# Transposes in rows of four, a gate ahead of the last product, and new due times in a planned convolution and MLP kernel

## The chip, the cores and the metric

The kernel runs on one core of a Trainium2 chip. Its time is the device time of one execution in microseconds, as the median of several runs. The profile comes from one more execution, taken by the hardware profiler. The engines are TensorE (PE; its weight loads are listed as PEld), VectorE (DVE), ScalarE (ACT), GpSimd (POOL) and SyncE (SP), which only starts transfers here.

## The reference

The input is a sequence of 2048 tokens with 640 channels. A layer norm with scale and shift goes into a gated long convolution (a short convolution of k by four taps, times v, then a causal convolution over all 2048 positions with a kernel for each channel, then times the normalised input), and its result is added to the input. A second layer norm with scale and shift goes into an MLP of width 1728 with a squared ReLU, whose result is gated and added:

```python
def _B_ref(x, w1, b1, w2, b2):
    h = jnp.einsum("bsd,df->bsf", x, w1) + b1
    zero = jnp.zeros_like(h)
    r = jnp.where(h > zero, h, zero)
    h = r * r
    out = jnp.einsum("bsf,fd->bsd", h, w2) + b2
    return out
...
h = _layernorm(x, axis=-1) * (1 + ca) + sa
x = x + ga * _A_ref(h, A_k, A_v, A_shift_k, A_ssm_k, A_ssm_D)
h = _layernorm(x, axis=-1) * (1 + cb) + sb
x = x + gb * _B_ref(h, B_w1, B_b1, B_w2, B_b2)
```

## The kernel before, in words

**Stages.** The convolution is done in five blocks of 128 channels, as transforms written as matrix products in float32. Its result x1 goes to DRAM (`x1_d`, in the trace `x_d`). The MLP follows. Its tokens are cut into eight chunks of 256 (n = 0 to 7), and two chunks form one of four pairs (s = 0 to 3). Every float32 operand of the MLP's products is split into a high and a low part of a faster float32 form (`split`: ACT copies the high part, DVE subtracts it), and a product is three matmuls (`l1`, 256 columns, and `l2`, 320 columns). A scheme with seven products in place of eight (sums and differences of blocks of the weights and the activations) saves matmuls in both layers. Layer one leaves its activations in DRAM (`h_d`); layer two loads them chunk by chunk, forms their differences, splits them into one of four buffers (in the trace `xp1r`, `ka`, `kz`, `xa`) and multiplies.

**The tokens** (`tokens`, `turned`). For each chunk x1 is loaded as two tiles of 128 tokens with 640 channels. They are normalised (`hat`), and each of the five blocks of 128 channels is transposed on PE: two transposes of 128x128 into one bank of PSUM (`xtp`), in two groups of their own, and one eviction by ACT (odd blocks) or DVE (even blocks), which applies scale and shift and writes the tile `xf`. From chunk 2 on the banks 6 and 7 serve for it. There are 80 such transposes.

**Layer two** (`second_layer`). In each chunk seven sums are built in seven banks (`ps7`, numbered 1 to 7), each from the six pairs of rows of the activations, p = 0 to 5; four of them (2, 4, 5 and 3) also get a remainder (rows a and c, with the bias). The result has four pieces: c[1,0] = ps2 + ps1, c[0,0] = ps4 + u3, c[0,1] = ps5 + u3 and c[1,1] = ps3 + u2, where u2 is first ps6 + ps1, u3 = ps7 + u2, and u2 then becomes ps5 + u2. Each piece is multiplied by the gate's row (`row0b`, in the trace `gbrow`), added to the residual (`xf` in the trace) and stored. In the last chunk, before, all four sums are formed first, and then the four pieces are gated, added and stored one after the other; c[1,1] is the last.

**What sets the order.** The program is first built as a graph of nodes, and a planner (`Graph.order`) then lays them on the engines: a simulated list schedule with a price for every node. On each engine the node that is ready and has the earliest due time goes next. The due times stand in a long table, `URGE`, in tenths of a microsecond with a minus sign, in the order in which the nodes of a kind are made; nodes of the MLP do not start earlier than a certain time before they are due. The instructions of each engine are then issued in this order, and on the chip each engine works its list strictly in this order, waiting for what an instruction needs. At most six transfers of SP are open at a time. For PE the planner prices a change of the form of a matmul (`ENTER`, `LEAVE`), where form was the number of rows and columns of the array in use, so that in the MLP before a transpose is no change of form. Only the order reaches the chip, no planned time does.

In the trace nearly all instructions carry the line L407, on which the planner issues them, so they are told apart by their tiles: `ps<-ident,x` and `ps<-ident,up` are the transposes of the tokens, `xf<-ps,cbs` their evictions, `ps<-t,w`, `ps<-xa,w`, `ps<-ka,w`, `ps<-kz,w` products of layer one, and `ps<-w,xp1r` and the like products of layer two.

## Time and profile before

| | us |
|---|---|
| median of 3 runs | 658.59 (658.23 to 659.29) |
| the profiled execution | 658.96 |
| its span | 657.2 |

The span runs from the first to the last instruction of the program in the profile; the execution's own time has 1.8 us more around it. The convolution takes PE up to about 280 us, layer one of the MLP up to about 477 us, layer two up to 652 us. "PE busy" counts matmuls as pipelined work with modelled ends, so durations of neighbours overlap; the cost of a matmul is read from one start to the next.

### The profile page before, as it was taken

Reading aid. Unit: us, or ns where it says so; the run is one execution under the profiler, and the core shown is the slowest. Engines: PE = TensorE matmul, PEld = TensorE weight load, DVE = VectorE, ACT = ScalarE, POOL = GpSimd, SP = SyncE. Lnnn points to the kernel's source line nnn. Section 1 sums busy time; section 2 is a strip of 40 time slices with the busy share of each in tenths; the row PEclk is TensorE's granted clock in tenths of the full one; section 3 lists DMA queues with packets and bytes.
Section 4 is the critical chain, followed back from the end, with each engine's and each line's share of the span. In section 5 each row is a group of like instructions: output and inputs, shape, how many; then the busy total and the mean of one; then the engine's idle time right before and its main releaser. Section 6 shows DMA issues by size and latency. Waiting matters only on the chain.

```text
span 657.2 us, 17277 instructions
## 1 busy us (share of the span) xinstructions
PE 629.6 (96%) x7012; PEld 584.4 (89%) x7012; DVE 516.1 (79%) x969; ACT 358.1 (54%) x681; POOL 226.8 (35%) x294
## 2 busy tenths in 40 slices
PE   7999999999999999899999999999989999999996
PEld 7888779878878878499999999999978999999996
DVE  1758848699978666886886787778899989788896
ACT  3554767885866775556585664456463424233321
POOL 1528649768786756311324200235400000000000
PEclk8999999999999999999999999999999999999999
DMA  9898989999896722563756632145555443553353
GB/s 223 217 272 284 267 231 249 208 234 216 229 241 164 142 56 72 156 208 89 213 152 194 193 112 75 56 140 166 159 147 171 151 137 118 166 176 120 114 157 81
DMA packets 143464, 111.00 MB, mean 169 GB/s; under 512 B 50836, under 2 KB 123348, under 8 KB 143384
## 3 DMA queue, kind: packets, MB, share of 16 engines
q1 hardware_dynamic: 141252, 109.28, 60.1%
q8 instruction: 55, 0.90, 0.6%
q10 hardware_dynamic: 2068, 0.61, 0.4%
q14 instruction: 25, 0.20, 0.1%
q0 software_dynamic: 64, 0.01, 0.0%
HBM read 79.99 MB, written 29.88 MB: 167 GB/s over the span
## 4 chain that ended last, share of the span: by engine, by line
PE 49%; DVE 3%; DMA 2%; ACT 1%; issue 1%; DVEq 0%; ACTq 0%
PE ps L407 49%; DMA up<-h_d 2%; DVE up L407 1%; DMA x<-x_d 1%; DVE w L407 0%; DVE ka L407 0%; DVE s L407 0%; DVE xp1r L407 0%; DVE kz L407 0%; ACT w L407 0%; ACT xf L407 0%; DVE xa L407 0%; DVE outs L407 0%; ACT kz L407 0%; ACT xa L407 0%
## 5 line engine op out<-in xcount | busy, mean ns | idle before, releaser
L407 PE MATMUL ps<-a,gb 128*64 128x128 f32 x1260 | 76.8, 275 | 3.3 <-ACT a L407 2.1
L407 PEld LDWEIGHTS ps<-a,gb 128*64 128x64 f32 x1260 | 69.3, 137 | 11.6 <-ACT a L407 5.4
L407 ACT ACTIVATE up<-ps,b1t 128x256 f32<-128x256 f32 (+1 forms) x112 | 50.6, 471 | 48.4 <-PE ps L407 46.4
L407 PE MATMUL ps<-t,w 128*128 128x256 f32 x504 | 72.7, 284 | 0.3 <-DVE up L407 0.3
L407 PEld LDWEIGHTS ps<-cst,p 64*64 64x64 f32 (+1 forms) x1792 | 60.7, 137 | 11.4 <-issue 6.1
L407 PE MATMUL ps<-cst,p 64*64 64x64 f32 (+1 forms) x1792 | 66.7, 247 | 3.9 <-POOL p L407 2.5
L407 PEld LDWEIGHTS ps<-t,w 128*128 128x128 f32 x504 | 64.8, 189 | 0.7 <-DVE up L407 0.5
L407 ACT ACTIVATE a<-ps 128x512 f32<-128x512 f32 x72 | 40.8, 620 | 31.9 <-PE ps L407 31.8
L407 DVE SCALAR_TENSOR_TENSOR up<-up 128x512 f32<-128x512 f32 (+2 forms) x70 | 45.3, 655 | 11.3 <-ACT up L407 10.6
L407 DVE TENSOR_TENSOR up<-up 128x256 f32<-128x256 f32 (+2 forms) x124 | 44.7, 383 | 7.4 <-DMA up<-h_d 5.7
L407 PE MATMUL ps<-xa,w 128*128 128x256 f32 x342 | 49.5, 284 | 0.0
L407 POOL TENSOR_TENSOR wm<-wm,wm 128x640 f32<-128x640 f32 x24 | 38.2, 1591 | 19.7 <-ACT wm L407 19.1
L407 PEld LDWEIGHTS ps<-xa,w 128*128 128x128 f32 x342 | 44.1, 190 | 0.4 <-DVE xa L407 0.2
L407 PE MATMUL ps<-w,xp1r 128*128 128x320 f32 x216 | 40.1, 310 | 1.9 <-ACT up L407 1.1
L407 PE MATMUL ps<-w,xa 128*128 128x320 f32 x216 | 41.1, 309 | 0.0
L407 PE MATMUL ps<-w,kz 128*128 128x320 f32 x216 | 39.9, 310 | 0.6 <-DVE kz L407 0.6
L407 PE MATMUL ps<-w,ka 128*128 128x320 f32 x216 | 40.4, 309 | 0.0
L407 DVE SCALAR_TENSOR_TENSOR kva<-ps,tap,kva 128x511 f32<-128x511 f32 (+2 forms) x48 | 35.8, 747 | 5.5 <-ACT kva L407 3.8
L407 DVE TENSOR_TENSOR up<-ps,up 128x256 f32<-128x256 f32 (+2 forms) x67 | 28.5, 435 | 13.4 <-PE ps L407 8.3
L407 PEld LDWEIGHTS ps<-w,xp1r 128*128 128x128 f32 x216 | 33.7, 188 | 2.6 <-ACT up L407 1.3
L407 PEld LDWEIGHTS ps<-w,kz 128*128 128x128 f32 x216 | 33.6, 188 | 1.0 <-DVE kz L407 1.0
L407 ACT ACTIVATE kz<-up 128x896 fp32r<-128x896 f32 (+2 forms) x24 | 16.8, 699 | 32.1 <-DVE up L407 31.8
(199 smaller groups left out, 1533.4 us busy)
## 6 DMA issues: line engine op xcount, KB each, us to landing
h_d<-up SPq DMA_DIRECT2D x51, 256.0 KB, 2.5
up<-h_d SPq DMA_DIRECT2D x48, 256.0 KB, 3.5
wm<-in_w_mod_dram SPq DMA_DIRECT2D x30, 320.0 KB, 5.2
w1s<-in_B_w_dram SPq DMA_DIRECT2D x25, 320.0 KB, 3.7
p<-in_A_ssm_k_dram SPq DMA_DIRECT2D x20, 256.0 KB, 4.4
p<-kv_d SPq DMA_DIRECT2D x20, 256.0 KB, 4.6
xp<-in_A_q_dram SPq DMA_DIRECT2D x10, 512.0 KB, 8.0
xf<-x_d SPq DMA_DIRECT2D x8, 640.0 KB, 4.1
```

Source lines behind the costliest of these rows:

```text
L407: fn(*real, **{k: a.real() if isinstance(a, View) else a for k, a in kw.items()})
```

## The change

It has three parts. First, from chunk 1 on, the blocks of a chunk's tokens are transposed as (0, 1), (2, 3) and (4): four transposes, or two for the last, as one node into one bank, which is then emptied by one eviction for each block. The form of a matmul in the MLP becomes the number of its entries in PE's queue, 4 for float32 and for transposes, 2 for the split products, and going from one to the other has a price in the planner, 0.040 and 0.085 us. Second, in the last chunk of layer two the pieces are gated as soon as their sums are there, and the last piece is taken apart: u2 is multiplied by the gate and added to the residual early, and ps3 is multiplied by the gate straight from its bank and added as the last step. `rest2` is the former inner loop as a function. Third, the table of due times is new: all of the MLP's, most of those of blocks 2 to 4 of the convolution, and some of blocks 0 and 1.

```diff
--- before.py
+++ after.py
@@ -30,8 +30,8 @@
 SPARE = 60.0
 
 FETCH = (3.6, 5.5)
-ENTER = {(64, 128): 0.104}
-LEAVE = {(64, 64): 0.11}
+ENTER = {(64, 128): 0.104, 4: 0.04, 2: 0.085}
+LEAVE = {(64, 64): 0.11, 4: 0.0, 2: 0.0}
 WINDOW = 10.24 / 3
 
 
@@ -679,10 +679,10 @@
     def mm(o, a, b, start, stop, hold=(), more=False):
         n = 2 if (isinstance(b, View) and b.buf.dtype == F32R) else 4
         ins = [x for x in (a, b) if isinstance(x, View)]
-        g.add("PE", 0.0, (nc.tensor.matmul, "matmul", (o, a, b), dict(start=start, stop=stop, **({"skip_group_check": True} if more else {}))), [o], ins, entries=n, hold=hold, form=(a.p[1] - a.p[0] if isinstance(a, View) else a.shape[0], o.p[1] - o.p[0]))
+        g.add("PE", 0.0, (nc.tensor.matmul, "matmul", (o, a, b), dict(start=start, stop=stop, **({"skip_group_check": True} if more else {}))), [o], ins, entries=n, hold=hold, form=(a.p[1] - a.p[0] if isinstance(a, View) else a.shape[0], o.p[1] - o.p[0]) if len(g.nodes) <= g.mlp else n)
 
     def turn(o, x, hold=()):
-        g.add("PE", 0.0, (nc.tensor.transpose, "transpose", (o, x, ident), {}), [o], [x] if isinstance(x, View) else [], entries=2, hold=hold, form=(P, P))
+        g.add("PE", 0.0, (nc.tensor.transpose, "transpose", (o, x, ident), {}), [o], [x] if isinstance(x, View) else [], entries=2, hold=hold, form=(P, P) if len(g.nodes) <= g.mlp else 4)
 
     def copy(eng, o, i, hold=()):
         if eng is act:
@@ -1220,19 +1220,23 @@
             out.append(o)
         return out
 
-    def turned(n, xh, b):
+    def turned(n, xh, bs):
         g.key = ("xt", n)
-        t = psum(f"xtp_{n}_{b}", (P, 2, P), XTB if n > 1 else (4, 5, 6, 7), **(one() if n > 1 else {}))
-        for i in range(2):
-            with g.as_one(0.11):
-                turn(t[:, i], xh[i][:, b * P : (b + 1) * P])
-        o = XF[n % 2][:, b]
-        t2 = t.rearrange("p i s -> p (i s)")
-        c1, c0 = cbs[:, 1, b : b + 1], cbs[:, 0, b : b + 1]
-        if b % 2:
-            act.activation(o, t2, AF.Identity, scale=c1, bias=c0)
-        else:
-            dve.tensor_scalar(o, t2, c1, c0, op0=ALU.mult, op1=ALU.add)
+        t = psum(f"xtp_{n}_{bs[0]}", (P, len(bs), 2, P), XTB if n > 1 else (4, 5, 6, 7), **(one() if n > 1 else {}))
+        turns = [(j, i) for i in range(2) for j in range(len(bs))]
+        for k in range(0, len(turns), len(turns) if n else 1):
+            some = turns[k:] if n else turns[k : k + 1]
+            with g.as_one(0.11 * len(some)):
+                for j, i in some:
+                    turn(t[:, j, i], xh[i][:, bs[j] * P : (bs[j] + 1) * P])
+        for j, b in enumerate(bs):
+            o = XF[n % 2][:, b]
+            t2 = t[:, j].rearrange("p i s -> p (i s)")
+            c1, c0 = cbs[:, 1, b : b + 1], cbs[:, 0, b : b + 1]
+            if b % 2:
+                act.activation(o, t2, AF.Identity, scale=c1, bias=c0)
+            else:
+                dve.tensor_scalar(o, t2, c1, c0, op0=ALU.mult, op1=ALU.add)
 
     def tokens(s, ks=(0, 1)):
         for k in ks:
@@ -1242,8 +1246,8 @@
             load_x1(n)
             stats2(n)
             xh = hat(n)
-            for b in range(NB):
-                turned(n, xh, b)
+            for bs in ((0, 1), (2, 3), (4,)) if n else ((b,) for b in range(NB)):
+                turned(n, xh, bs)
             if k == 0:
                 halves(n, T1[s])
 
@@ -1521,6 +1525,17 @@
             for i, (a, y) in enumerate(((0, 0), (0, 1), (1, 0))):
                 mm(acc, h[a], w[y], first and i == 0, last and i == 2)
 
+    def rest2(n, ps7, i):
+        k, o = {2: (1, 0), 4: (0, 0), 5: (0, 1), 3: (2, 1)}[i]
+        g.key = ("l2", n)
+        a, c = HS[n, "a"], HS[n, "c"]
+        wa, wc = W2S[NF - 2], W2S[NF - 1]
+        o = slice(320 * o, 320 * o + 320)
+        l2(ps7[i], parts(a, k), (wa[:, 0, o], wa[:, 1, o]), False, False)
+        with g.as_one(0.294):
+            mm(ps7[i], c[:, k], wc[:, 0, o], False, False)
+            mm(ps7[i], cone[n % 2][:, k], wc[:, 1, o], False, False)
+
     def second_layer(n):
         x = X2[n] = xres[n % 2]
         ps7 = {i: psum(f"c{i}_{n}", (P, 320), ANY, track=f"c{(7 * n + j) % 8}") for j, i in enumerate((1, 2, 6, 7, 4, 5, 3))}
@@ -1542,15 +1557,8 @@
                 wv = parts(w, b) if b < 6 else (e[:, 0], e[:, 1])
                 l2(ps7[i], parts(h, a), wv, p == 0, p == NP - 1)
             if p == 4:
-                g.key = ("l2", n)
-                a, c = HS[n, "a"], HS[n, "c"]
-                wa, wc = W2S[NF - 2], W2S[NF - 1]
-                for i, k, o in ((2, 1, 0), (4, 0, 0), (5, 0, 1), (3, 2, 1)):
-                    o = slice(320 * o, 320 * o + 320)
-                    l2(ps7[i], parts(a, k), (wa[:, 0, o], wa[:, 1, o]), False, False)
-                    with g.as_one(0.294):
-                        mm(ps7[i], c[:, k], wc[:, 0, o], False, False)
-                        mm(ps7[i], cone[n % 2][:, k], wc[:, 1, o], False, False)
+                for i in (2, 4, 5, 3):
+                    rest2(n, ps7, i)
             if p == 2:
                 g.key = ("lx2", n)
                 rows = x1_d.buf.real[n * CH : (n + 1) * CH, :].rearrange("(l p) d -> p l d", p=P)
@@ -1562,11 +1570,11 @@
         add(dve, c[:, 1, 0], ps7[2], e1)
         add(dve, u2, ps7[6], e1)
         add(dve, u3, ps7[7], u2)
-        add(dve, c[:, 0, 0], ps7[4], u3)
-        add(dve, u2, ps7[5], u2)
-        add(dve, c[:, 0, 1], ps7[5], u3)
-        add(dve, c[:, 1, 1], ps7[3], u2)
         if n < NC - 1:
+            add(dve, c[:, 0, 0], ps7[4], u3)
+            add(dve, u2, ps7[5], u2)
+            add(dve, c[:, 0, 1], ps7[5], u3)
+            add(dve, c[:, 1, 1], ps7[3], u2)
             for i in range(2):
                 t = c[:, i].rearrange("p k d -> p (k d)")
                 mul(dve, t, t, row0b)
@@ -1574,477 +1582,480 @@
             for a in range(2):
                 sp_dma(osrc[a, :, 2 * n : 2 * n + 2], x[64 * a : 64 * a + 64], 5120)
             return
-        for i, k in ((1, 0), (0, 0), (0, 1), (1, 1)):
+
+        def gated(i, k, t, done=True):
             o = slice(320 * k, 320 * k + 320)
-            mul(dve, c[:, i, k], c[:, i, k], row0b[:, o])
+            mul(dve, c[:, i, k], t, row0b[:, o])
             add(dve, x[:, i, o], x[:, i, o], c[:, i, k])
-            for a in range(2):
+            for a in range(2) if done else ():
                 (act_dma if a else sp_dma)(osrc[a, :, 2 * n + i, o], x[64 * a : 64 * a + 64, i, o], 1280)
 
+        gated(1, 0, c[:, 1, 0])
+        add(dve, c[:, 0, 0], ps7[4], u3)
+        gated(0, 0, c[:, 0, 0])
+        add(dve, u2, ps7[5], u2)
+        gated(1, 1, u2, False)
+        add(dve, c[:, 0, 1], ps7[5], u3)
+        gated(0, 1, c[:, 0, 1])
+        gated(1, 1, ps7[3])
+
     URGE = {
...
-        ("hat", 0): [-1183, -2159],
+        ("hat", 0): [2106, -32],
...
+        ("l2", 7): [-6306, -5775, -7408, -6254, -6504, -5644, -6237, -8084, -5259, -5995, -7115, -6238, -6310, -6026,
+            -6324, -6350, -6191, -6322, -6400, -6434, -7376, -6077, -6318, -6221, -6411, -6487, -6320, -6275, -5914,
+            -6078, -6349, -5864, -7141, -6229, -7236, -6205, -6317, -7217, -7128, -6343, -6013, -6351, -6279, -6050,
+            -6223, -6030, -6160, -6511, -6402, -5611],
...
-        ("lw2", 0): [-3968],
...
+        ("lw2", 0): [-3539],
...
```

In the row for the products of the last chunk (`l2`, 7) the first 35 numbers are pairs 0 to 4, seven each in the order 1, 2, 6, 7, 4, 5, 3 of the sums; then come the remainders of 2, 4, 5 and 3, two numbers each; the last seven are pair 5. The due times of the loads of layer two's weights moved from 396.8, 362.0, 396.6 and 393.2 us to 353.9, 329.4, 351.4 and 365.9 for the first four tiles, and others of them moved later.

200 lines of the change are left out of this document (100 added, 100 removed), and 655 rows, old and new, of the table URGE.

## The prediction

> **What bounds the kernel now.** I read the page first, then the table of stages, then TensorE's line of time at the stages where it idles, then the transposes, and last the end of the chain.
>
> ```profile
> PE 629.6 (96%) x7012; PEld 584.4 (89%) x7012; DVE 516.1 (79%) x969; ACT 358.1 (54%) x681; POOL 226.8 (35%) x294
> ```
>
> TensorE (PE) is busy for 629.6 of 657.2 us. An edit pays only where it takes work or a wait away from PE, or shortens what comes after PE's last product. Where PE still idles stands in the table by stage (length, then busy time by engine, clock, DMA share):
>
> ```profile
> core 0: us, PE busy (x) PEld busy (x) DVE busy (x) ACT busy (x) POOL busy (x), PEclk, DMA share, GB/s
> 262.00:280.00 18.00, 14.05 (x97) 7.83 (x93) 15.14 (x29) 10.45 (x19) 7.08 (x7) 1.00 0.58 161
> 280.00:477.00 197.00, 195.54 (x1616) 192.60 (x1616) 155.16 (x326) 114.50 (x249) 52.30 (x51) 1.00 0.47 147
> 477.00:500.00 23.00, 19.28 (x125) 17.95 (x124) 21.24 (x46) 12.07 (x20) 0.23 (x1) 1.00 0.55 166
> 500.00:652.20 152.20, 152.12 (x1038) 151.68 (x1036) 133.16 (x241) 51.17 (x71) 0.00 (x0) 1.00 0.45 138
> 652.20:657.20 5.00, 0.00 (x0) 0.00 (x0) 1.43 (x3) 0.00 (x0) 0.00 (x0) 0.91 0.26 66
> ...
> 130.00:262.00 132.00, 126.76 (x2484) 1.00 0.71 167
> ```
>
> The clock is full throughout. Idle time of PE: 5.2 us in the later blocks of the convolution (130 to 262, a row of a second such table), 3.95 us where the convolution hands over to the MLP (262 to 280), 1.5 us in the first layer, 3.7 us where the first layer hands over to the second (477 to 500), 0.1 us in the second layer, and the 5.0 us after the last product. So a new order of the MLP can gain at the two handovers, 7.7 us together; in the layers themselves it can only lose. The large waits in the handovers, from PE's line of time (the bracket is the idle time before the row and what ended it):
>
> ```profile
> 263.06 2.06 PE L407 MATMUL ps<-gi,wxa 64*128 64x128 f32 x32 [0.77 <-ACT q L407]
> 266.92 1.50 PE L407 MATMUL ps<-ident,q 128*128 128x128 f32 x12 [1.81 <-DVE q L407]
> ...
> 478.29 0.71 PE L407 MATMUL ps<-w,xp1r 128*128 128x320 f32 x3 [0.80 <-DVE up L407]
> 480.42 0.71 PE L407 MATMUL ps<-w,xp1r 128*128 128x320 f32 x3 [1.07 <-ACT up L407]
> 499.05 0.41 PE L407 MATMUL ps<-s,kz 128*128 128x320 f32 x1 [1.23 <-DVE kz L407]
> ```
>
> Five waits, 5.68 us together, 1.14 us each in the mean. All end with VectorE (DVE) or ScalarE (ACT). In 477 to 500 DVE is busy for 21.24 of 23 us: it converts the last weights of layer two, evicts the last sums of layer one and splits the first activations of layer two, all at once. An order that converts weights earlier, in the first layer where DVE idles for 41.8 of 197 us, relieves it; this is the one large thing that a new order can do.
>
> **Part 1: transposes in rows of four.** A run of transposes between products, from PE's line of time (start, length, name, count):
>
> ```profile
> 302.99 1.93 PE L407 MATMUL ps<-xa,w 128*128 128x256 f32 x15
> 304.76 0.60 PE L407 MATMUL ps<-ident,x 128*128 128x128 f32 x4
> ...
> 374.60 0.38 PE L407 MATMUL ps<-ident,x 128*128 128x128 f32 x2
> 374.73 0.95 PE L407 MATMUL ps<-t,w 128*128 128x256 f32 x6
> 375.52 0.27 PE L407 MATMUL ps<-ident,x 128*128 128x128 f32 x1
> 375.55 0.96 PE L407 MATMUL ps<-t,w 128*128 128x256 f32 x6
> 376.35 1.22 PE L407 MATMUL ps<-xa,s 128*128 128x256 f32 x9
> ...
> 408.60 0.60 PE L407 MATMUL ps<-ident,x 128*128 128x128 f32 x4
> 408.96 0.95 PE L407 MATMUL ps<-t,w 128*128 128x256 f32 x6
> 409.75 0.53 PE L407 MATMUL ps<-ident,x 128*128 128x128 f32 x3
> ...
> L407 PE MATMUL ps<-ident,x x60: 270/272/328, 304.8 to 411.2; 128*128 128x128 f32 x60
> ```
>
> Products follow each other at (304.76 - 302.99) / 15 = 0.118 us, so six take 0.71. One transpose with six products takes 376.35 - 375.52 = 0.83 us, two take 375.52 - 374.60 = 0.92, four take 409.75 - 408.60 = 1.15. Less the products that is 0.12, 0.21 and 0.44: 0.11 us for each transpose and at most 0.01 for going in and out of a run. The changed planner prices a run at 0.040 to enter and 0.085 to leave; PE does not pay that. The 60 transposes of chunks 2 to 7 lie in 26 runs now (I counted them on the line of time) and need 18 in rows of four: 8 runs fewer are 8 x 0.01 = 0.1 us by the trace, 8 x 0.125 = 1.0 us by the planner's price. I take -0.1, since the rows are of these very transposes.
>
> What a row costs: it needs both normalised halves and a whole bank, and two evictions leave that bank.
>
> ```profile
> L407 DVE TENSOR_SCALAR xf<-ps,cbs x24: 491/538/547, 278.2 to 412.3; 128x256 f32<-128x256 f32 x24
> L407 ACT ACTIVATE xf<-ps,cbs x16: 548/566/567, 278.4 to 410.2; 128x256 f32<-128x256 f32 x16
> ...
> 371.67 0.56 ACT L407 ACTIVATE xf<-ps,cbs 128x256 f32<-128x256 f32 x1 [0.63 <-PE ps L407]
> 371.99 0.54 DVE L407 TENSOR_SCALAR xf<-ps,cbs 128x256 f32<-128x256 f32 x1
> ```
>
> Now the two engines empty two banks side by side (at 371.99 they overlap). Seven chunks with two full rows each make 14 pairs of evictions out of one bank. If the second has to wait for the first, that is up to 14 x 0.54 = 7.5 us of waiting on ACT or DVE, with the other evictions and splits queued behind it. In the first layer DVE idles for 41.8 us and ACT for 82.5, so I put it at 0 on PE; without that cover it costs 0.54 us a chunk. [...]
>
> **Part 2: the last chunk's sum.** DVE's line at the end, with PE's last product:
>
> ```profile
> 649.02 0.49 DVE L407 TENSOR_TENSOR outs<-outs,gbrow 128x320 f32<-128x320 f32 x1
> 649.54 0.49 DVE L407 TENSOR_TENSOR xf<-xf,outs 128x320 f32<-128x320 f32 x1
> 649.95 1.08 DVE L407 TENSOR_TENSOR outs<-ps,outs 128x320 f32<-128x320 f32 x2
> ...
> 651.07 0.49 DVE L407 TENSOR_TENSOR outs<-outs,gbrow 128x320 f32<-128x320 f32 x1
> 651.52 0.60 PE L407 MATMUL ps<-s,xa 128*128 128x320 f32 x3
> 651.59 0.49 DVE L407 TENSOR_TENSOR xf<-xf,outs 128x320 f32<-128x320 f32 x1
> 652.16 0.49 DVE L407 TENSOR_TENSOR outs<-ps,outs 128x320 f32<-128x320 f32 x1
> 652.68 0.49 DVE L407 TENSOR_TENSOR outs<-outs,gbrow 128x320 f32<-128x320 f32 x1
> 653.21 0.49 DVE L407 TENSOR_TENSOR xf<-xf,outs 128x320 f32<-128x320 f32 x1
> ```
>
> After the last product three steps of DVE follow, 652.16 to 653.70, then the store. The change leaves two of them: the product with the gate reads the bank itself. One step is 652.68 - 652.16 = 0.52 us. In return two steps (u2 by the gate, and its addition) come in ahead of the last product. DVE works without a break from 649.02 to 652.08, so with PE's order as it is they would push it to 653.1, the two last steps would end at 654.2, and the tail would be 0.5 us longer. They are free only if the product for ps5, which u2 needs, ends about 1 us further ahead of the last one. In the new due times of the last chunk ps5's last product is due at 640.2, while the fifth product of ps4 is due at 714.1 and that of ps3 at 723.6, each with its remainder and its last product behind it, so ps5 should be done well before both. I take -0.5; the ends are -0.5 and +0.5. ACT's and SP's stores of the other pieces lie under PE's last products as before.
>
> **Part 3: the new order.** The due times of the whole MLP and of blocks 2 to 4 of the convolution are new; what is computed is the same. The profile of before cannot show the new order. Bounds from the rows: at best all five large waits go, -5.7; at worst nothing goes and new ones come, in stages that have almost none. Several weights of layer two have earlier due times, which fits the overfull DVE at 477 to 500; the second layer's have moved both ways. I take one wait of the five gone in the balance, -1.1, nearer to the low end than to the middle, because the same order also disturbs 350 us in which PE waits for only 1.6 us. The later blocks of the convolution I put at 0: they have 5.2 us of waits to lose and 126.8 us of full work to disturb.
>
> **Sum.** -0.1 - 0.5 - 1.1 = -1.7 us. The profiled execution took 658.96 us, 657.2 of it span and 1.8 around it; it lies 0.4 us above the median 658.59 of the three runs shown. The sum on its span gives 655.5, on the median 656.9. About 0.2% (1.3 us) is what a measurement of this kernel can tell from no change.
>
> **Rivals.**
> - *The waits only change places.* For it: PE's waits are short and many, and each engine's queue is in order, so one removed often shows the next. Against: DVE's spare time lies just before the handover that lacks it. Then parts 1 and 2 stay alone: 658.59 - 0.6 = 658.0.
> - *Layer two starves (slower).* There PE runs 152.12 of 152.2 us and DVE 133.16: per chunk of 19.0 us DVE has only 2.4 us to spare. The splits of each pair follow a load:
>
> ```profile
> 497.53 0.89 DVE L407 TENSOR_TENSOR up<-up 128x256 f32<-128x256 f32 x2 [1.05 <-DMA up<-h_d]
> 498.44 0.55 DVE L407 TENSOR_TENSOR kz<-up,kz 64x384 fp32r<-64x384 f32 x1
> ```
>
>   Here DVE waited 1.05 us for a load, and PE 1.23 us for what came of it. If the new order lets loads or splits come so late, more than DVE's 2.4 us in a chunk, PE stops. Two such stops are +2.5, with the tail's -0.5: 660.6. Against it: before has no such wait after 500.
> - *The shared bank (slower).* If the second eviction of a row is on PE's path once in each of seven chunks: 7 x 0.54 = +3.8, less 0.5: 661.9. [...]
> - *The planner's price is right*, and rows of four save 1.0 us, with the tail and nothing else: 657.1. The three runs of transposes above speak against it.
>
> **How the numbers follow.** The forecast, at least one wait gone: 0.45 at 656.9. Waits change places: 0.27 at 658.0 (no difference). Starved second layer: 0.17 at 660.6. Shared bank: 0.06 at 661.9. Price right: 0.05 at 657.1. So faster 0.45 + 0.05 = 0.50, same 0.27, slower 0.17 + 0.06 = 0.23. The range reaches down to four waits of the five gone (658.59 - 0.6 - 4 x 1.14 = 653.4) and up past two new stops with a little of a worse tail: 661.0. The forecast's own range is 653.4 to 657.3.
>
> **What would show it.** Right: runs of four transposes that still cost 0.44 us and no run cheaper than 0.11 for each transpose; two steps of DVE after the last product, store at about 653.2 less what PE gained; PE's idle time in 262 to 280 and 477 to 500 under 7.7 us by one to several us, with DVE less crowded at 477 to 500. Wrong: waits of PE for DVE or for loads in the second layer; evictions of a row that follow each other with PE idle behind them; three steps of DVE or more after the last product; or more idle time in 130 to 262.

## The result and the profile after

| | before | after |
|---|---|---|
| first comparison, median | 659.36 (6 runs, 658.23 to 661.75) | 663.96 (6 runs, 662.83 to 665.97) |
| ratio, 95% interval | | 1.0069 [1.005, 1.0087] |
| repeated later, median | 659.06 (23 runs) | 665.16 (6 runs), 1.0108 [1.0078, 1.0138] |
| the profiled execution, its span | 658.96, 657.2 | 662.83, 660.7 |

The change makes the kernel slower, by 4.6 us in the first comparison and 6.1 in the repeat. The forecast was 656.9, so it was wrong in sign; the result also lies above the upper end of its range, 661.0. The profiled execution of after is the fastest of its six and carries 3.5 us of the loss in its span; the repeat's profile (run e8) has to stand beside it.

The table by stage of the kernel after, cut as the table of before (length, then busy time by engine, clock, DMA share, GB/s):

```profile
130.00:262.00 132.00, 124.46 (x2460) 107.43 (x2460) 100.13 (x163) 87.33 (x175) 90.76 (x117) 0.99 0.66 158
262.00:280.00 18.00, 13.99 (x101) 7.75 (x98) 12.93 (x26) 9.58 (x18) 3.29 (x4) 1.00 0.63 185
280.00:477.00 197.00, 194.97 (x1598) 191.09 (x1599) 156.24 (x327) 113.49 (x251) 50.98 (x51) 1.00 0.46 145
477.00:500.00 23.00, 20.60 (x133) 20.10 (x131) 19.29 (x43) 11.54 (x19) 2.61 (x3) 0.93 0.55 172
500.00:652.00 152.00, 150.25 (x1023) 149.98 (x1023) 132.20 (x240) 51.69 (x72) 0.00 (x0) 1.00 0.47 140
```

PE idles 7.5 us in 130 to 262 (5.2 before), 4.0 in 262 to 280 (3.95), 2.0 in 280 to 477 (1.5), 2.4 in 477 to 500 (3.7) and 1.75 in 500 to 652 (0.1). DVE is less crowded at 477 to 500, 19.29 in place of 21.24 us, as forecast, but PE gains nothing by it: a wait of 1.55 us now stands behind 500 us, and a stretch at half clock counts as busy. And the clock is no longer full: 0.93 in 477 to 500, 0.99 in 130 to 262. Between 100 us and the last product PE's clock was granted at half for 3.41 us twice (lengths and columns as above):

```profile
484.51:487.92 3.41, 3.41 (x15) 3.41 (x14) 3.07 (x7) 0.25 (x1) 0.00 (x0) 0.50 0.94 262
221.68:225.10 3.42, 3.42 (x51) 3.30 (x45) 2.65 (x3) 1.13 (x3) 1.87 (x2) 0.50 0.64 142
```

**The handover from layer one to layer two.** PE's waits from 475 us to the end, summed by what ended them (us in total, times, longest), of before and of after:

```profile
PE ps L407 <- DVE kz L407: 1.8, 2, 1.2
PE ps L407 <- ACT up L407: 1.1, 1, 1.1
PE ps L407 <- DVE up L407: 0.8, 1, 0.8
```

```profile
PE ps L407 <- ACT up L407: 2.4, 1, 2.4
PE ps L407 <- DVE s L407: 1.6, 1, 1.6
PE ps L407 <- DVE ka L407: 0.2, 1, 0.2
```

They were 3.7 us and are 4.2: fewer waits, longer ones. How the longest comes about, from the line of time of after:

```profile
478.94 2.81 DVE L407 TENSOR_TENSOR up<-up 128x128 f32<-128x128 f32 x8 [1.77 <-DMA up<-h_d]
480.72 0.95 ACT L407 ACTIVATE ka<-up 128x896 fp32r<-128x896 f32 x1 [2.11 <-DVE up L407]
481.58 0.72 ACT L407 ACTIVATE s<-w2s 128x640 fp32r<-128x640 f32 x1
482.32 0.97 ACT L407 ACTIVATE up<-ps,b1t 64x256 f32<-64x256 f32 x2
483.35 0.71 PE L407 MATMUL ps<-w,xp1r 128*128 128x320 f32 x3 [2.40 <-ACT up L407]
...
502.31 0.41 PE L407 MATMUL ps<-s,cones 128*128 128x320 f32 x1 [1.55 <-DVE s L407]
```

Read upwards from the row at 483.35: PE waits 2.40 us for a bank that the last evictions of layer one (482.32) have to empty. They stand in ACT's queue behind a weight's split (481.58) and the split of `ka`, and the latter waited 2.11 us for DVE's differences, which waited 1.77 us for a load. No engine was slow; three queues in a fixed order passed a load's delay on to PE. The last row is the wait behind 500 us.

**The rows of four.** PE's line of time at the transposes of two chunks in after:

```profile
370.78 1.03 PE L407 MATMUL ps<-ident,x 128*128 128x128 f32 x8
371.57 0.96 PE L407 MATMUL ps<-ka,w 128*128 128x256 f32 x6
372.62 0.44 PE L407 MATMUL ps<-ident,x 128*128 128x128 f32 x2
372.81 0.96 PE L407 MATMUL ps<-t,w 128*128 128x256 f32 x6
373.73 1.39 PE L407 MATMUL ps<-ident,x 128*128 128x128 f32 x8
374.88 0.96 PE L407 MATMUL ps<-t,w 128*128 128x256 f32 x6
375.80 0.44 PE L407 MATMUL ps<-ident,x 128*128 128x128 f32 x2
375.99 0.96 PE L407 MATMUL ps<-t,w 128*128 128x256 f32 x6
```

The first line is two rows of four, one directly behind the other. They don't wait: counted to the second product behind them, as the first product of a run starts a little early, the eight transposes take 0.88 us, 0.11 each. From start to start they take 371.57 - 370.78 = 0.79, and six products up to a run that doesn't wait take 0.79 too (e5's lines below: 368.88 - 368.09). The pair behind them starts 372.62 - 371.57 = 1.05 after six products began, so 0.26 late. The next eight start 373.73 - 372.81 = 0.92 after six products began, 0.13 late, and take 374.88 - 373.73 = 1.15, which is 0.36 more than the first eight. These are waits for a bank. Each row holds one until both its evictions are done, and those run one after the other (ACT, then DVE, of the same bank):

```profile
371.42 0.56 ACT L407 ACTIVATE xf<-ps,cbs 128x256 f32<-128x256 f32 x1 [0.35 <-PE ps L407]
372.02 1.00 DVE L407 TENSOR_SCALAR xf<-ps,cbs 128x256 f32<-128x256 f32 x2 [1.62 <-ACT xf L407]
```

DVE stood 1.62 us for ACT here; no run here shows what would happen without that wait. Summed over the 70 transposes of chunks 1 to 7, the time from the product before each run to the second product behind it, less 0.11 us for each transpose and less the products, is 0.50 us in before and 2.16 in after. I call this the excess. In after the groups of chunks 2 to 7 take the banks 6 and 7 in turn; a group waits there while rows that stand close before it still hold both.

**The convolution.** PE's waits in 100 to 280 us that nothing shown ends (the profile's "issue"), before and then after:

```profile
PE ps L407 <- issue: 1.0, 2, 0.7
```

```profile
PE ps L407 <- issue: 3.3, 3, 2.2
```

The longest of after, and what its DMA queues moved between 218.5 and 221.4 us (queue, packets, MB, share):

```profile
221.38 0.91 PE L407 MATMUL ps<-cst,p 64*64 64x64 f32 x30 [2.16 <-issue]
```

```profile
q8 instruction: 1, 0.02, 2.9%
```

One packet of 16 KB on the queue `q8 instruction`, which starts at 218.60; PE goes on 2.78 us later. The other two such waits of after, 0.24 us up to 229.92 and 0.93 us up to 233.71, end 2.30 and 2.64 us after a packet of this queue starts (227.62 and 231.07), and the two of before, 0.28 us up to 221.82 and 0.72 us up to 226.52, end 2.44 and 2.53 us after one (219.38 and 223.99). Between 100 and 280 us either trace has 24 such packets, so most have no such wait behind them. That PE was waiting for its own instructions is my reading of this; no run shows it. I call these waits issue waits.

**The tail.** In after:

```profile
655.56 0.60 PE L407 MATMUL ps<-w,xa 128*128 128x320 f32 x3
656.20 0.49 DVE L407 TENSOR_TENSOR outs<-ps,gbrow 128x320 f32<-128x320 f32 x1
656.72 0.49 DVE L407 TENSOR_TENSOR xf<-xf,outs 128x320 f32<-128x320 f32 x1
```

Two steps behind the last product, as forecast. It ends at 656.16, so 4.53 us of the span lie behind it; before it ended at 652.12, with 5.07 behind.

### The profile page after: what moved, and what is told of

Its sections match the earlier page's. It is cut to its first block, busy times and chain, and to the rows that moved or that the text cites. A ratio compares the mean times of both kernels' runs of the same rounds, so it can differ in the third digit from the quotient of the medians.

```text
span 660.7 us, 17267 instructions
## 1 busy us (share of the span) xinstructions
PE 630.8 (95%) x7012; PEld 588.3 (89%) x7012; DVE 511.5 (77%) x970; ACT 356.4 (54%) x681; POOL 220.7 (33%) x294
## 4 chain that ended last, share of the span: by engine, by line
PE 70%; DMA 9%; DVE 9%; ACT 4%; issue 3%; POOL 2%; SPq 1%; ACTq 0%; DVEq 0%; POOLq 0%
PE ps L407 70%; DVE up L407 2%; DMA wm<-in_w_mod_dram 2%; DMA up<-h_d 2%; DMA p<-in_A_ssm_k_dram 2%; DVE kva L407 2%; DMA w1s<-in_B_w_dram 1%; SPq L618 1%; DMA d<-in_A_ssm_D_dram 1%; DVE kacc L407 1%; DVE w L407 1%; POOL wxa L407 1%; DMA kv_d<-kacc 1%; ACT w L407 1%; DVE xf L407 0%
## 5 line engine op out<-in xcount | busy, mean ns | idle before, releaser
L407 PEld LDWEIGHTS ps<-cst,p 64*64 64x64 f32 (+1 forms) x1792 | 59.1, 136 | 12.9 <-issue 9.2
L407 PE MATMUL ps<-cst,p 64*64 64x64 f32 (+1 forms) x1792 | 64.6, 245 | 5.0 <-issue 3.3
L407 DVE SCALAR_TENSOR_TENSOR up<-up 128x512 f32<-128x512 f32 (+3 forms) x70 | 46.4, 673 | 2.6 <-ACT up L407 2.1
L407 PEld LDWEIGHTS ps<-w,ka 128*128 128x128 f32 x216 | 35.1, 194 | 0.5 <-DVE ka L407 0.5
L407 ACT ACTIVATE xp1r<-up 128x896 fp32r<-128x896 f32 (+1 forms) x16 | 13.5, 844 | 40.4 <-DVE up L407 33.2
```

The lines of the kernel that those rows point to most:

```text
L407: fn(*real, **{k: a.real() if isinstance(a, View) else a for k, a in kw.items()})
```

## The experiments

Eighteen kernels were run, in five groups, each beside runs of the kernel before. In most of them the planner was replaced by a list: each engine issues its instructions in the order of before or of after, with the moves named. Such a list fixes the order but, except in e16, e17 and e18, not which of several free places a tile gets: e7 and e9 to e12 differ from their parent in five or six tiles of the convolution, e6 in two tiles of layer two as well, e2 to e5 and e13 to e15 also in banks of the layers. This became part of the answer. e1 is before's program in all but DVE's last steps, e18 in all but the end of the last chunk, and e8 is after's, so they also show how much two executions of the same instructions differ.

**e1, the tail alone.** The planner with the due times of before; PE's order is unchanged.

```diff
+gated(1, 0, c[:, 1, 0]); add(dve, c[:, 0, 0], ps7[4], u3); gated(0, 0, c[:, 0, 0])
...
+gated(1, 1, u2, False); ... ; gated(1, 1, ps7[3])
```

> The kernel before with the second edit alone (last chunk's sum gated ahead of its last product), in the order of before on every engine but for the last steps of DVE; the last product of PE stays the one of ps4, so three steps of DVE still stand behind it, and DVE has one step more. Theory A (the loss lies in the new order, at the change from layer one to layer two and in convolution blocks 2 to 4): 658.6 to 659.1, that is 0 to +0.5, since the edit gains only where ps3's product comes last. Theory B (the rows of four cost, through the shared bank): the same here. Theory C (the edit itself costs, through its additional step and its order of the stores): +1 or more, 659.7 and up.

660.18 us (12 runs; before 659.24), ratio 1.0013 [0.9996, 1.003]. No gain that can be told: the median lies in theory C's range, but the interval holds 1. 5.44 us lie behind the last product in place of 5.07, so without a new order on PE the edit gives nothing and makes the tail 0.37 longer, as the prediction had said of PE's order as it is (0.5). This profile shows something else: with before's order and banks its waits at the handover are 1.44 and 2.10 us (at 480.02 and 483.19), with 6.83 us at half clock behind them.

**e2, rows alone, and e5, the same rows at another place.** Both have before's order on every engine. In e2 a row stands where its second block's transposes stood, in e5 where its first block's did; the evictions stay where they were.

```diff
-PE: T(0) ... T(1) ...        DVE: ... evict(0) ...   ACT: ... evict(1) ...
+PE (e2): ... T(0,1) ...      at the place of T(1)
+PE (e5): T(0,1) ...          at the place of T(0)
```

> The kernel before with the first edit alone: transposes of the tokens of chunks 1 to 7 in rows of four in one shared bank, everything else in the order of before. Theory A (the loss is in the new order): 658.4 to 659.2, that is -0.2 to +0.5, the windows of PE at 477 to 500 and 500 to 652 us as before. Theory B (a shared bank is late to come free, both evictions must end): +2 to +4, 660.6 to 662.6, with more idle time of PE in 130 to 262 and 500 to 652 us, ended by DVE or ACT at the transposes. No half-speed window of the clock in theory A.

> As e2 (rows of four alone in the order of before), but each row stands where its first block's transposes stood, not where its second block's did; in e2 the eviction of the first block kept its place on DVE or ACT and so had to wait there for the later row, with everything behind it. Theory A (rows cost only where an in-order queue waits for them): most of e2's +16 goes, 659 to 663, with DVE's idle time before the evictions xf<-ps,cbs back near that of before. Theory B (one bank for two blocks is held too long in any order): still 668 or more, with PE's waits in 280 to 480 us ended by xf evictions.

e2: 675.54 (6 runs), 1.0254 [1.0222, 1.0286], far above both theories. e5: 659.71 (12 runs; before 659.06), 1.0018 [1.0003, 1.0034]. e2's convolution is before's (last product 277.48 us); all is lost in layer one. Its line of time:

```profile
315.37 0.54 DVE L419 TENSOR_SCALAR xf<-ps,cbs 128x256 f32<-128x256 f32 x1 [1.94 <-PE ps L419]
...
320.44 0.54 DVE L419 TENSOR_SCALAR xf<-ps,cbs 128x256 f32<-128x256 f32 x1
...
321.01 0.56 ACT L419 ACTIVATE xf<-ps,cbs 128x256 f32<-128x256 f32 x1 [0.38 <-DVE xf L419]
...
321.63 0.95 PE L419 MATMUL ps<-xa,s 128*128 128x256 f32 x6 [2.79 <-ACT xf L419]
```

The first eviction keeps its place on DVE and now has to wait there for a later row (1.94 us), with everything behind it; then PE waits 2.79 us for the bank, which is free only after the second eviction at 321.01. With the row at the first block's place nearly all of it is gone; what is left, 0.65 us, is small, but its interval lies above 1. The two kernels also differ in 50 banks of layer one; e13 and e16 below show such a difference, in 32 banks, to be worth some 2 us, so most of the 16 us hangs on one position in a queue. (This made e2 look like the shared bank's proof, which it is not.)

**e3 and e4, splices by kind.** Before's MLP order with after's convolution order, and the reverse.

```diff
-URGE of one kernel for all kinds
+e3: after's for the convolution, before's for the MLP;  e4: the reverse
```

> The code of before with the convolution's work in the order of after and the MLP's work in its order of before, spliced (so the joint is not the same as in either parent). Theory A in its first form (convolution blocks 2 to 4 lose about 1.1 us by the last convolution product, the change from layer one to layer two loses the other 2.4): 659.5 to 660.5, the last convolution product at about 278.5 us. In its second form (all of it at the change of layers): 658.5 to 659. A rival (the splice itself makes new waits): over 661 with waits at places that neither parent has. Theory B: as before, 658.6.

> The code of after and its MLP order, with the convolution's work in the order of before, spliced. Theory A in its first form (convolution 1.1 us, change of layers 2.4 us, with a half-speed window of the clock at about 484 us): 662 to 663, the window at 484 still there. In its second form (all at the change of layers): 663 to 664. Theory B (rows of four): 663 to 664 too, with PE's idle time at the transposes. If it comes out at 660 or less, the loss is made in the convolution and only shows later.

680.82 and 672.17 us: misses of both forms, and what e3's rival said, that the splice itself makes new waits. In the window from 130 to 280 us both kinds of work share every queue, and each order seems to fit only its own partner (e4 has a wait of 3.85 us at 173.6 and one of 3.60 at 272.4 that neither parent has). They tell nothing of where after loses.

**e6, two of after's long waits mended.**

```diff
 ACT at 173:  -wm<-wm,sg  up<-xp  a<-ps  a<-ps        +a<-ps  a<-ps  wm<-wm,sg  up<-xp
 ACT at 482:  -ka<-up  s<-w2s  up<-ps,b1t (two)       +ka<-up  up<-ps,b1t (two)  s<-w2s
 DVE at 482:  -up<-up (square)  ka<-up,ka             +ka<-up,ka  up<-up (square)
```

> The kernel after with two small moves in its order. On ACT at about 482 us the last two layer-one evictions go ahead of a weight split, and on DVE the second part of the ka split ahead of a squaring; on ACT at about 172 us two copies of a bank go ahead of a modulation's product and a normalisation. Theory A (the loss of after is a few long waits of PE that the order makes, one at the change of layers with the half-speed window behind it): the wait at 483 falls from 2.40 to about 1.7 us and, where the half-speed window at 484 goes with it, 1.7 us more; the wait at 174 falls from 1.24 to about 0: 661 to 663, that is -1 to -3 against after. Theory D (the waits only change places): 663.5 to 664.5, the saved time comes back as other waits within 20 us.

668.49 (4 runs), 1.016 [1.0136, 1.0183]: slower by 3 us than after again. Its waits from 475 us:

```profile
PE ps L419 <- DVE xa L419: 2.1, 1, 2.1
PE ps L419 <- ACT up L419: 1.7, 2, 1.5
PE ps L419 <- DVE s L419: 1.6, 1, 1.6
PE ps L419 <- ACT xa L419: 0.9, 1, 0.9
```

The wait at 483 fell from 2.40 to 1.51 as worked out, and 2.95 us of new ones came ten microseconds later, where the next buffer (`xa`) is split. At 174 the wait for ACT was gone, and an issue wait of 0.95 us stood at the same place. This is theory D, that they change places, though it came out 4 us above its range.

**e7, the tail with ps3's product last.** As e1, with the last three groups of ps3 behind those of ps4.

```diff
-PE: ... ra:3 rc:3 p5:3 | p2:4 p3:4 p4:4 ra:4 rc:4 p5:4
+PE: ... p2:4 p3:4 p4:4 ra:4 rc:4 p5:4 | ra:3 rc:3 p5:3
```

> The kernel before with the second edit, as in e1, and with the last four products of ps3 moved behind those of ps4 on PE, so that two steps of DVE stand behind the last product in place of three; everything else in the order of before. If the tail edit is worth what the trace of after shows for it (span less end of the last product 4.53 in place of 5.07 us): -0.5 against e1 and -0.5 to 0 against before, 658.5 to 659.5, span less end of the last product at 4.5 to 4.6 us. If moving ps3's products makes a wait of its own (its bank or its operands late): 660 or more, with a wait of PE in the last 4 us.

659.76 (12 runs), 1.0003 [0.9984, 1.0022]. Behind the last product lie 5.23 us, not 4.5: only 1.18 us of products separate ps4's end from ps3's, and DVE's three steps for ps4 (0.52 us each) are not done when ps3 is. See e18.

**e8, after once more.** No edit.

> The kernel after once more, as a control with a second profile. Theory A: 663.5 to 664.5, the wait of about 2.4 us at 483 us there again and the last conv product at 277.5 to 279.5 us; the half-speed window at 484 may or may not be there, as the wait falls within one window of the clock or over two. If the waits of the first profile were chance, other places carry the loss.

665.16 (6 runs). The wait at the handover is there (2.13 us at 484.43), another of 1.76 at 493.35, and three half-speed windows, at 176.5, 268.7 and 494.0 us. The first profile was no accident. Its last convolution product starts at 279.69 us, 1.1 later than in the first profile.

**e9, e10, e11, e12: the two costs of a wait.** In e9 a store goes behind two loads in SP's queue; in e10, 16 products whose result nothing reads fill the wait at 483; e11 is both; e12 fills before's two waits at 478 and 480 with 13 such products.

```diff
 SP at 210 (e9, e11):  -kv_d<-kva  xp<-in_A_q (two)  p<-kv_d    +xp<-in_A_q (two)  kv_d<-kva  p<-kv_d
+PE at 481 (e10, e11): for _ in range(16): mm(spare, h, w[:, 0:192], False, False)
```

> The kernel after with one move in SP's queue at about 210 us: the last store of k and v of the fourth convolution block goes behind the two 512 KB loads of xp, as in before, in place of ahead of them. In after the four 256 KB loads p<-kv_d then started at 214.0 us on top of xp's transfer, and PE stood 2.16 us at 221.4 us for nothing but its own instructions, with a half-speed window behind it; in before they started at 220.5 us. Theory E (the part of the loss that lies in the convolution is PE's instruction supply behind a burst of loads): the loads start at about 216 to 219 us, the unexplained waits of PE in 100 to 280 us fall from 2.6-3.3 to 0.4-2 us, 662 to 663.3, that is -1 to -2 against after. Against it: the loads only come later and PE waits for p instead, 664 or more.

> The kernel after with 16 additional products of 128x192 on PE, into columns of an accumulator's bank that nothing reads, inside the wait at 483 us; they end before the wait does. Theory F (the long wait costs twice, once as a wait and again through the half-speed window that follows a window of 3.41 us in which PE stood for over half): the half-speed window at 484 is gone, -1 to -1.7 in the executions that had it, 662.3 to 663.5 in the median; the granted clock higher by 0.002 to 0.003. If the clock is set by something else: 664 as after, or 0.3 more where the products run over the wait's end.

> e9 and e10 together. Theories E and F: their gains add, 660.5 to 662.5, the granted clock of most executions at 0.996 or more. What then still stands above before is the remaining wait at the change of layers and what else of the new order costs. If neither holds: 664.

> The kernel before with 13 additional products of 128x192 inside its two waits at 478.3 and 480.4 us (five in the first, eight in the second), nothing else changed. Theory F: its executions at a granted clock of 0.991 to 0.992, which lay at 661.5 to 663.4, become rare; the median falls by 0 to 0.7, 658.3 to 659.2. Against it: the products delay the ones behind them by 0.2 to 0.5 and nothing is gained, 659.3 to 659.8.

e9: 665.47 (6 runs), 1.0095 [1.0062, 1.0127]; e10: 665.18, 1.008 [1.0056, 1.0105]; e11: 664.39, 1.0086 [1.0053, 1.012]; e12: 659.75 (12 runs; before 658.78), 1.001 [0.9997, 1.0023]. In e9 the loads start at 218.84 in place of 214.02 us, yet PE stands as long in issue waits (4.0 us in five, against 3.3 and 2.6 in after's two profiles), so theory E fails as a remedy. The last convolution product is early in e9 and e11 (277.06, 277.40), where theory E would have it, but the whole is not faster. In e10 PE is busy through the wait and the half-speed window at 484 is gone; but the next wait, 1.76 us for `xa`, has one behind it at 494.6. The times don't move. e12 agrees with theory F about the clock: all its twelve executions were granted 0.997 or more, while 56 of 101 executions of before had less. It shows no gain in time, and does not separate whether the windows cost little in before or the added products cost as much as they save.

**e13, e14, e15: everything but the new order, and the new order cut in time at 276 us of the plan.**

```diff
 e13: -before's pairs, before's tail     +rows as in e5, tail as in e7, order of before
 e14: e13 with after's order until 276;  e15: e13 with after's order from 276
```

> The first two parts of the change together (rows of four, each at its first block's place, and the tail with ps3's product last) in the order of before: everything but the new order. Theory A (the whole loss is the new order's): 658.5 to 660.0, within 0.2% of before, PE's transposes and layer-one products in the second half 0.3 to 0.5 us cheaper than before's, span less end of the last product 4.5 to 5.2 us. If the parts cost something together that neither showed alone: 661 or more.

> As e13, but with the order of after for all that after's plan starts before the last convolution product is done (276 us in the plan), and the order of before for the rest; a cut in time, not by kind as e3 and e4 were. Five profiles in each order put the end of the last convolution product at about 277 us (before's order) and 279 us (after's), and the rest at 375 and 378 us. Theory A1 (both halves of the new order lose, 2 and 3 us): 661 to 662.5, last convolution product at 278 to 280 us, the rest at 374.5 to 376. Theory A2 (only the layers lose): 659 to 660. If the joint itself makes waits: over 664, with waits of PE at 276 to 300 us that neither has.

> The counterpart of e14: the order of before until 276 us, the order of after for the rest. Theory A1: 661.5 to 663, last convolution product at 276 to 277.5 us, the rest at 377 to 379 us, with a half-speed window of the clock near 484 to 495 us in most executions. Theory A2 (only the layers lose): 663 to 665. Theory A3 (only the convolution's half loses, and the layers' loss is its consequence): 659 to 660. If the joint itself makes waits: over 665, with waits at 276 to 300 us.

e13: 662.41 (6 runs; before 659.27), 1.0051 [1.0035, 1.0067]; e14: 672.59, 1.0193 [1.0163, 1.0224]; e15: 662.85, 1.0061 [1.0043, 1.0079]. e15 says that the layers' part of the change, with rows and tail in it, costs 3.6 us: theory A1, with the rest (defined in the table below) at 378.91 us, though the last convolution product came at 278.85, later than forecast. It does not say that the new order costs 3.6, since e13 loses 3.1 without it; e16 below, with better banks, loses 0.7. e14 has after's issue waits (6.8 us) and a joint with three waits of its own (0.71, 1.75 and 0.73 us at 284.8, 287.0 and 288.2), so it gives no clean number for the convolution's part. e13 was the surprise: e5's rows and e7's tail in e5's order, and 2.7 us slower than e5 (2.5 when each is taken against its own runs of before). Its line of time at the transposes, then e5's at the same place:

```profile
369.30 0.95 PE L419 MATMUL ps<-t,w 128*128 128x256 f32 x6
370.78 0.66 PE L419 MATMUL ps<-ident,x 128*128 128x128 f32 x4 [0.53 <-DVE xf L419]
371.19 0.95 PE L419 MATMUL ps<-kz,w 128*128 128x256 f32 x6
372.67 0.44 PE L419 MATMUL ps<-ident,x 128*128 128x128 f32 x2 [0.53 <-DVE xf L419]
```

```profile
368.09 0.95 PE L419 MATMUL ps<-t,w 128*128 128x256 f32 x6
368.88 0.60 PE L419 MATMUL ps<-ident,x 128*128 128x128 f32 x4
369.24 0.96 PE L419 MATMUL ps<-kz,w 128*128 128x256 f32 x6
370.04 0.38 PE L419 MATMUL ps<-ident,x 128*128 128x128 f32 x2
```

The same instructions in the same order. In e13 the second row of this chunk was given the bank of the first, bank 6 for both, and the fifth block's pair too, so each has to wait for two evictions; in e5 they take turns with bank 7. The excess is 2.27 us in e13 and 0.56 in e5.

**e16, e13 with the banks of e5.** The edit is that alone: 32 banks, of which three are of groups of transposes (one is shown) and 29 of sums of layer one.

```diff
-e13, chunk 4: row (0,1) bank 6, row (2,3) bank 6, pair (4) bank 6
+e16, chunk 4: row (0,1) bank 6, row (2,3) bank 7, pair (4) bank 6
```

> e13 with the same order on every engine, but with the banks of e5: there the last pair of a chunk (its fifth block) mostly goes into the bank that the second row doesn't hold back, while in e13 it often goes into the bank of a row that is still being evicted. In e13 (and e14, which has its banks) PE lost 2.27 us at the transposes of chunks 1 to 7 over 0.11 us for each transpose, in e5 0.56, in before 0.50. Theory G (a row holds its bank until both its evictions are done, and what the rows cost is the wait of the next group for that bank): the excess falls back to about 0.6 us, 659.5 to 660.8, that is -1.6 to -2.9 against e13. If e13's loss was elsewhere (its wait of 2.43 us at 481 us): the excess falls and the time stays at 661.5 to 662.5.

660.37 (12 runs; before 659.65), 1.0012 [0.9993, 1.003]. The loss against before falls from 3.1 to 0.7 us, the excess from 2.27 to 1.14. By the profile 0.4 us of the 0.7 lies behind the last product (5.45 us, with e7's tail). Theory G holds for the rows: what they cost is the wait of the next group for a bank that two evictions hold. The excess explains half of the 2.4 us. The longest wait at the handover fell with it, from 2.43 to 1.13 us at nearly the same sum (3.74 and 3.58), and with it went the 6.83 us at half clock that e13's profile has behind that wait; this run does not separate these, nor the three banks from the 29.

**e17, after with five groups of transposes two or three products later.**

```diff
-PE: T4(0..3) l1 l1 T4(4) l1 l1 T5(0,1) T5(2,3) l1 l1 T5(4) l1 ...
+PE: T4(0..3) l1 l1 l1 l1 T4(4) T5(0,1) l1 l1 T5(2,3) l1 ...
```

> The kernel after, in its own banks, with five groups of transposes of chunks 4, 5 and 7 two or three layer-one products later on PE, behind the evictions that they wait for at 372 to 376 and 402 us; nothing else moved. Theory G: PE's excess at the transposes of chunks 1 to 7 falls from 1.8-2.4 to 0.7-1.2 us, and the time by as much, 662.5 to 664. If DVE and ACT, in whose queues the evictions keep their places, now wait for the later transposes and give the time back: 664 or more, with the excess down and new waits of layer-one products within some us.

667.42 (6 runs), 1.0114 [1.0075, 1.0153]. A miss: the excess stayed at 1.97 us. At 372 to 378 it fell from 0.96 to 0.71, at 402 it stayed, and at the last group, 410 to 414, it grew from 0.17 to 0.57; and the `xa` wait grew to 3.65 us with two half-speed windows behind it. In this kernel no wait of after could be moved alone.

**e18, the tail with ps3 far enough behind.** As e7, in before's own banks, with five groups of ps3 (2.1 us) behind ps4.

```diff
-PE: ... ra:3 rc:3 p5:3 | p2:4 p3:4 p4:4 ra:4 rc:4 p5:4
+PE: ... p2:4 p3:4 p4:4 ra:4 rc:4 p5:4 | p3:3 p4:3 ra:3 rc:3 p5:3
```

> The kernel before, in its own banks and order, with the second edit, and with the last five groups of ps3's products behind all of ps4's on PE. In e7 only three groups (1.18 us) stood between ps4's end and ps3's; DVE's three steps for ps4 still ran when ps3 was done, and 5.23 us lay behind the last product in place of 4.53 in after. Here some 2.1 us lie between the two. If the tail edit is worth what after's trace shows: the span less the end of the last product at 4.5 to 4.6 us, 657.7 to 659, that is -0.5 against before, the only version here that should beat it, by less than the measurement tells surely. If ps4's products, now earlier, make waits: 659.5 or more, with a wait of PE in the last 5 us.

659.21 (12 runs; before 659.38), 0.9993 [0.9981, 1.0006]. Its end:

```profile
653.11 0.60 PE L419 MATMUL ps<-w,xa 128*128 128x320 f32 x3
653.17 0.49 DVE L419 TENSOR_TENSOR xf<-xf,outs 128x320 f32<-128x320 f32 x1
653.75 0.49 DVE L419 TENSOR_TENSOR outs<-ps,gbrow 128x320 f32<-128x320 f32 x1
654.27 0.49 DVE L419 TENSOR_TENSOR xf<-xf,outs 128x320 f32<-128x320 f32 x1
```

The last product ends at 653.71, 4.53 us before the end: the tail edit's 0.54 us is there in before's order too. It has the lowest ratio of all versions. That it beats before is not shown, since the interval holds 1.

## Why the prediction was wrong

Six profiles side by side (us; "rest" is from the last convolution product's start to the end of the last product of all; half-speed windows from 100 us on, before and after the last convolution product):

| profile | last convolution product | issue waits, 100 to 280 | rest | excess | waits from 475 | half-speed windows | behind the last product |
|---|---|---|---|---|---|---|---|
| before | 277.46 | 1.0 | 374.66 | 0.50 | 3.7 | 0, 0 | 5.07 |
| e5 | 275.99 | 1.5 | 374.38 | 0.56 | 3.7 | 0, 0 | 5.07 |
| e16 | 277.10 | 0 | 375.13 | 1.14 | 3.6 | 0, 0 | 5.45 |
| after | 278.58 | 3.3 | 377.58 | 2.16 | 4.2 | 1, 1 | 4.53 |
| e8 | 279.69 | 2.6 | 378.01 | 1.76 | 4.4 | 2, 1 | 4.53 |
| e15 | 278.85 | 1.9 | 378.91 | 2.43 | 5.3 | 0, 1 | 4.54 |

Layers: the rest is 374.7 in the mean of the upper three and 378.2 of the lower, +3.4 us: +1.4 of excess, +1.0 of waits from 475 us, and some 0.8, an estimate, for a half-speed window (e7, which has one and before's rows, has a rest of 375.44, before one of 374.66); some 0.3 is not accounted for. Convolution: ten profiles with before's order (before, e1, e2, e5, e7, e12, e13, e15, e16, e18) start its last product at 277.4 in the mean, eight with after's (after, e6, e8 to e11, e14, e17) at 279.6, +2.3 us; the issue waits are 1.4 and 4.6 us, and half-speed windows are none against eight. Tail: -0.5. Together +5.2, against 664.63, the median of after's twelve runs, less 659.25, that of all of before's: +5.4.

That this comes close to the total is in part luck, since single executions differ by as much as its terms. The upper three are profiles without a half-speed window. Before, e1 and e18 are the same program up to the last chunk, and their rests are 374.66, 377.12 and 375.59 us; e1 has two half-speed windows, e18 has none. Over before, e1, e5, e7, e16 and e18 against after, e8, e9 and e15 the rest differs by 3.1 us. In the convolution e6, e9 and e11 carry an edit of their own and e14's joint lies at its end; before, e1 and e18 against after, e8 and e17, each three times the same program there, differ by 1.5 us. What holds beyond this is that the two groups do not overlap: the waits from 475 us sum to 3.5 to 4.0 us in nine profiles with before's order and to 4.2 to 6.0 in five with after's whose waits are neither filled nor mended (the splices e3, e4 and e14 left aside); the issue waits are 0 to 2.3 us in the ten and 2.6 to 6.8 in the eight.

- **Part 1, a run of transposes at 0.11 us each and the planner's price not paid: right.** Runs of four that wait for nothing cost 0.44 us.
- **Part 1, "a row costs two evictions out of one bank, 0 on PE": wrong.** I weighed it by the idle time of ACT and DVE in the whole of layer one. But PE does not need an engine with time; it needs one of two banks, now, and a row keeps it for two evictions (0.56 and 0.50 us in the rows of after above) where a pair kept it for one. The rival with this mechanism had the right cause at 0.06, with too high a price; the excess is 1.4 us more (the rival's 3.8 assumed a wait of 0.54 in each of seven chunks, and there were six visible ones in all, of 0.17 to 0.55). That a row can cost nearly nothing is also true, at e5's places and banks.
- **Part 2, the tail: right,** -0.54 against -0.5 behind the last product. The condition that ps5 be done early enough held in after's order, and e7 shows what happens where such a condition fails.
- **Part 3, "one wait of the five gone in the balance, -1.1": this is the step that failed.** At 262 to 280 nothing changed (3.95 and 4.01 us of idle time), and from 475 us the waits grew, 3.7 to 4.2, 4.4 and 5.3 us. The sign that I had named came true all the same, 6.4 us of idle time in the two stretches in place of 7.7, but only because one wait moved past 500 us and half-clock time counts as busy. DVE did become less crowded at 477 to 500, as the step assumed; but PE did not wait less for it. In after's trace a load of the first activations and the order of ACT's and DVE's queues set the longest wait, and in e6 and e17 what was taken from one wait came back at a later one. My own rival "the waits only change places" described the mechanism, but put its price at zero: the waits' sum grew by some 1.0 us, and a half-speed window behind a long one costs more, by the estimate above some 0.8. Long waits are not the new order's alone (e1 and e13 have them in before's order), but every profile of the new order whose waits are neither filled nor mended has one of over 2 us. How much of the layers' loss is the order and how much the banks that the planner gave with it stays open: e15 has both.
- **Part 3, "the later blocks of the convolution I put at 0": wrong,** +1.5 to +2.3 us. I saw no issue wait worth a row in before's trace (1.0 us in two) and did not ask what the new order would do to these waits. That these waits belong to the new order is shown by eight profiles against ten; why it has more of them is not. e9 speaks against the burst of loads as the sole cause. The planner's code has a term `FETCH` that can hold PE up and a term `rate` that can halve its speed; I used neither.
- **Rival "layer two starves":** right sign, wrong place. PE waited 1.55 us at 502.31 for the weights with the bias, whose row was loaded at 496.77 in place of 481.73 in before, at the handover's end; in the rest of layer two nothing stops.

## What to carry to other kernels

When a change lets one bank serve two evictions, count the banks that are free in the next microsecond, not the idle time of the engines that empty them; which banks a kernel with the same order gets was worth 2 us here (e13 and e16). Of waits between in-order queues, ask what stands behind the one removed (in e6 one wait lost 0.89 us, and 2.95 us of new ones came); a forecast that "one of five goes" needs the name of the one and of its successor. Test a new order by its longest wait as well as by the sum, and in more than one execution: the same program's waits at one place were 1.2 us at most in one profile and 2.1 in another.

## What was not expected of the hardware

**Half-speed windows.** In after's trace PE's clock was granted at half twice from 100 us on, at 221.68 to 225.10 and 484.51 to 487.92 us. In the 3.41 us just before (218.27 to 221.68 and 481.10 to 484.51) PE idled for 2.16 and 2.25 us. Of the other stretches of 3.41 us from 100 us to the last product, counted on in equal steps from these two, the one with the most idle time has 1.91 us (266.06 to 269.47); in before, counted from its half-speed window at 11.15 us, it has 1.81 (263.73 to 267.15). Behind both the clock was full. The length of the wait alone does not tell: in e8 the wait of 2.13 us that ends at 484.43 has no half-speed window behind it, and the one of 1.76 that ends at 493.35 has one at 494.0. What the granted clock goes by is not shown. At a granted clock of 0.998 or more before took 658.8 us in the mean of 38 executions, and after 662.6 in the only one of its twelve, so by this one execution some 4 us of the loss stand without the clock; in another, at 0.987, after took 669.7.

**Issue waits.** The five of before and after between 100 and 280 us, of 0.24 to 2.16 us, end 2.30 to 2.78 us after a packet of 16 KB on `q8 instruction` starts, and all five stand ahead of the convolution's products of 64x64 (`ps<-cst,p`). What PE waited for is not shown.
